# A change of token order inside a batch, so that three rows of q, k and v lie together for a partition

## The chip, the cores and the metric

The kernel runs on one core of one Trainium2 chip, in one launch. The metric is the device time of that core in microseconds (us), a median over runs. A core has five engines with an instruction stream each: TensorE (PE in the profile, with its weight loads as PEld), VectorE (DVE), ScalarE (ACT), GpSimd (POOL) and SyncE (SP). In this kernel SP issues every DMA, one after the other, in the order of its instruction stream; its rows are called SPq.

## The reference

Attention over 4 batches of 12 heads, 448 tokens and 64 dimensions, and then two feed-forward layers on 1792 tokens of 768 features. Cut to what matters:

```python
q_n, k_n = rmsnorm(q, g_q), rmsnorm(k, g_k)          # over the 64 dimensions of a head
scores = q_n @ k_n.transpose(0, 1, 3, 2) / sqrt(64)   # 448 x 448 for each head
attn = softmax(scores)
x = (attn @ v).transpose(0, 2, 1, 3).reshape(1792, 768)
h = x @ w_in                                          # 768 -> 2048
x = (h * sigmoid(1.702 * h)) @ w_out                  # 2048 -> 768
h = x @ w_in2
out = (max(h, 0) + alpha * min(h, 0)) @ w_out2
```

All is in float32. A token's row of the output depends on the tokens of its batch through a sum over keys, so the tokens of a batch may stand in any order as long as q, k and v have the same one and the output rows go back to their places.

## The kernel before

Products are formed from float16 halves: a float32 value becomes a high and a low part, and three matmuls (high by high, high by low, low by high) stand for one. The work goes by pairs of heads, 6 pairs in a batch (NP), 24 in all; P counts them.

For a pair, `load_qk` (L312) brings q and k of both heads into one tile `qk` of 128 partitions by 7 places by 2 heads by 64 numbers. 448 tokens are three and a half blocks of 128, so k takes places 0 to 2 and the lower half of place 3, and q the upper half of place 3 and places 4 to 6. Token 128c + p lies in place c on partition p. A head needs four DMAs (three blocks of k, the rest of k, three blocks of q, the rest of q), a pair eight. In batches 1 to 3 the second head's q begins 64 tokens late and ends with its first 64. `load_v` (L329) brings v in five DMAs: three blocks, the last 64 rows, and the first 64 rows once more. `normalize` (L350) squares on ACT (`sq`, L362), sums and takes the inverse root on DVE, and scales on DVE for the first eight pairs and on POOL for the rest (L379, L380). `prep_pair` (L383) makes the high and the low half (`hl`, L393 on ACT, L394), and one DMA transpose (L399) turns them into `t1`, in which tokens run along the columns. For batches 1 to 3 it also splits v into `vs` and copies two pieces of it to other partitions (L413, L414).

A pair has four units of up to 128 query rows for each head. `scores` (L450, tile `sp`, two buffers in PSUM) is followed by the row maximum on DVE (`nm`, L452) and the exponential on ACT (`pr`, L461). In batch 0 the probabilities are turned by float32 matmuls with a diagonal (`tp`, L494) and copied out by ACT (`ptf`, L497). In batches 1 to 3 they are split into halves (`ph`, L479 on ACT, L502 on DVE) and turned by DMA transposes (L508) into `pt`. The fourth unit of a pair has 64 rows of each head in one tile. `values` (L525, tile `xp`) multiplies by v; in batch 0 the second half of a pair goes in three parts of 192, 128 and 64 columns for each block of keys, in the other batches in two.

The stages follow each other in time. The first stage runs the first two units of all six pairs of batch 0, between the loading and conversion of the first weights (`weights`, L180, loads at L200, conversions at L132, L148, L149, splits at L163, L164). `first_x` and `first_in` (L620) then begin the first layer for batch 0, while the last two units of each pair follow. Then the first layer's second half (`yp`, L690) and the batches 1 to 3 (`hp`, L667) run on PE, with the attention of the next batch woven in by a fixed pace (L1094 to L1105). The second layer (`h`, L775, and `op`, L931) and the stores (L923) end the program. `v_scale` (L279) reads all of v of a batch in eight loads (`vst`) for a common scale; for batch 1 it is called at step 8 (VS_AT) of the second loop over batch 0, L1075.

What sets the order on each engine is a scheduler that simulates the program when it is built: each engine's stream is then fixed. So an edit that shortens one thing moves others too.

## Time and profile before

| | us |
|---|---|
| median of 3 runs | 1238.12 (1235.25 to 1238.38) |
| the profiled execution | 1238.87, span 1237.1 |
| PE busy | 1091.2 (88% of the span) |
| DVE busy | 845.0 (68%) |
| ACT busy | 708.2 (57%) |
| POOL busy | 84.1 (7%) |
| DMA queue that SP issues to | 302480 packets, 159.45 MB, 50.4% of the time of 16 DMA engines |

The span is the time from the first instruction to the last. PE's share is an average over stages with different limits: in the slices of the page it is at nine tenths or more from the middle of the program on, and far below that at the beginning. Busy time doesn't count the issuing of DMAs, so SP has no line in the table; its issues stand in the timeline as SPq rows with a start and a length.

### The profile page before, as it was taken

To read this page: it belongs to the slowest core of one execution; us is meant where nothing else is said; L and a number is where in the kernel's file an instruction comes from. 1 tells how busy PE (TensorE), PEld (TensorE's weight loads), DVE (VectorE), ACT (ScalarE), POOL (GpSimd) and SP (SyncE) were. 2 spreads that over 40 slices of the span, in tenths; PEclk is the share of its full clock that TensorE was granted. 3 is DMA by queue.
4 is the path that set the end of the run, shared out by engine and by line. 5 is a ranking of instruction groups with operands and counts; after the bars stand their busy time and mean duration, and the time that the engine had idled before them with its cause. 6 is when DMAs were issued, how large, how long until landed. Compare 5 with 4: busy or idle time off the path is not lost.

```text
span 1237.1 us, 18887 instructions
## 1 busy us (share of the span) xinstructions
PE 1091.2 (88%) x6877; PEld 615.3 (50%) x6877; DVE 845.0 (68%) x1594; ACT 708.2 (57%) x1447; POOL 84.1 (7%) x54
## 2 busy tenths in 40 slices
PE   0564589976988889899999999799999999999998
PEld 0332357765544444445545555444444458666665
DVE  6988868899666687646764295749997334777441
ACT  2673767787567776656876256236766535565220
POOL 0000000032122123211100000000000000000000
PEclk9886789997999999899999999999999999999999
DMA  6784724466677757675655470346534214352200
GB/s 161 201 217 134 185 78 121 113 115 120 140 153 145 146 116 155 131 124 107 117 99 106 144 263 1 115 176 221 198 134 165 75 73 139 115 165 93 69 33 32
DMA packets 302573, 160.65 MB, mean 130 GB/s; under 512 B 240272, under 2 KB 285840, under 8 KB 302480
## 3 DMA queue, kind: packets, MB, share of 16 engines
q1 hardware_dynamic: 302480, 159.45, 50.4%
q8 instruction: 54, 0.88, 0.3%
q14 instruction: 39, 0.32, 0.1%
HBM read 92.02 MB, written 25.69 MB: 95 GB/s over the span
## 4 chain that ended last, share of the span: by engine, by line
PE 53%; DVE 20%; DMA 11%; ACT 8%; issue 5%; SPq 4%; DVEq 0%; ACTq 0%
PE op L931 15%; PE yp L690 12%; PE h L775 9%; PE hp L667 7%; PE xp L525 4%; PE sp L450 3%; DVE nm L452 2%; ACT pr L461 2%; PE tp L494 2%; PE hp L620 2%; DVE ph L502 2%; DMA t<-hl 2%; DMA g<-in_moe_w_in_dram 1%; DVE g L125 1%; DMA g<-in_moe_w_out_dram 1%
## 5 line engine op out<-in xcount | busy, mean ns | idle before, releaser
L690 PE MATMUL yp<-g,w1o 128*128 128x448 f16 x1152 | 231.1, 359 | 0.5 <-DVE g L125 0.3
L775 PE MATMUL h<-x,w2i 128*128 128x512 f16 (+1 forms) x1152 | 218.9, 352 | 0.9 <-ACT neg L782 0.9
L667 PE MATMUL hp<-x,w1i 128*128 128x448 f16 x864 | 172.6, 358 | 2.5 <-ACT x L124 1.6
L690 PEld LDWEIGHTS <-w1o 128*128 128x128 f16 x1152 | 111.7, 99 | 116.7 <-issue 19.8
L775 PEld LDWEIGHTS <-w2i 128*128 128x128 f16 x1152 | 112.6, 98 | 106.1 <-issue 1.2
L667 PEld LDWEIGHTS <-w1i 128*128 128x128 f16 x864 | 83.2, 99 | 86.8 <-issue 14.0
L461 ACT ACTIVATE pr<-sp,nm,c_s 128x448 f32<-128x448 f32 x168 | 120.3, 719 | 2.0
L502 DVE SCALAR_TENSOR_TENSOR ph<-pr,sm,ph 128x448 f16<-128x448 f32 x126 | 95.2, 782 | 19.7 <-ACT ph L479 19.6
L450 PE MATMUL sp<-t 64*128 64x448 f16 (+1 forms) x480 | 61.3, 364 | 42.5 <-ACT pr L461 21.2
L452 DVE TENSOR_REDUCE nm<-sp 128x2 f32<-128x896 f32 x96 | 92.5, 964 | 7.8 <-PE sp L450 7.4
L931 PEld LDWEIGHTS <-even 128*128 128x128 f16 x672 | 65.7, 98 | 43.1
L479 ACT ACTIVATE ph<-pr,sm 128x448 f16<-128x448 f32 x126 | 77.8, 659 | 14.8 <-DVE sm L470 13.4
L783 DVE SCALAR_TENSOR_TENSOR pos<-neg,nalpha,pos 128x512 f32<-128x512 f32 (+1 forms) x64 | 43.5, 681 | 61.0 <-ACT neg L782 60.8
L781 ACT ACTIVATE pos<-h 128x512 f32<-128x512 f32 (+1 forms) x64 | 34.4, 538 | 70.6 <-PE h L775 66.4
L494 PE MATMUL tp<-dg,pr 128*128 128x128 f32 x336 | 56.6, 328 | 15.1 <-ACT sq L362 7.5
L620 PE MATMUL hp<-x,w1i 128*128 128x256 f16 (+1 forms) x576 | 62.1, 266 | 7.3 <-DVE t L632 4.2
L931 PEld LDWEIGHTS <-odd 128*128 128x128 f16 x504 | 49.3, 98 | 32.6
L125 DVE SCALAR_TENSOR_TENSOR g<-t,ratio_w1o,g 128x448 f16<-128x448 f32 x64 | 51.4, 805 | 20.4 <-ACT g L124 20.0
L931 PE MATMUL op<-w2lo,even 128*128 128x384 f16 x384 | 63.5, 326 | 0.0
L494 PEld LDWEIGHTS tp<-dg,pr 128*128 128x128 f32 x336 | 50.4, 233 | 25.3 <-issue 10.9
L620 PEld LDWEIGHTS <-w1i 128*128 128x128 f16 x576 | 53.3, 101 | 15.4 <-issue 11.6
L362 ACT ACTIVATE sq<-qk 128x448 f32<-128x448 f32 x48 | 27.3, 574 | 57.2 <-DMA qk<-in_k_dram 29.0
(201 smaller groups left out, 1606.1 us busy)
## 6 DMA issues: line engine op xcount, KB each, us to landing
g<-in_moe_w_in_dram SPq DMA_DIRECT2D x24, 512.0 KB, 5.2
g<-in_moe_w_out_dram SPq DMA_DIRECT2D x32, 384.0 KB, 3.8
w2raw<-in_moe_w_in_dram SPq DMA_DIRECT2D x24, 512.0 KB, 5.3
w2raw<-in_moe_w_out_dram SPq DMA_DIRECT2D x16, 768.0 KB, 6.3
g_dram<-pos SPq DMA_DIRECT2D x48, 256.0 KB, 2.0
gp<-g_dram SPq DMA_DIRECT2D x8, 1024.0 KB, 6.7
odd<-g_dram SPq DMA_DIRECT2D x6, 1024.0 KB, 5.5
y_dram<-y SPq DMA_DIRECT2D x24, 224.0 KB, 2.3
```

The source lines that it names most:

```text
L125: nc.vector.scalar_tensor_tensor(out=dst[1], in0=src, scalar=scale, in1=dst[0], op0=ALU.mult, op1=ALU.subtract)
L450: nc.tensor.matmul(out=dst, lhsT=lhsT, rhs=kt[ds, 0:S], start=(i == 0), stop=(i == 2))
L452: nc.vector.tensor_reduce(out=nm[:, 0:n], in_=sp[:, 0:n, 0:S], op=ALU.max, axis=AX, negate=True)
L461: nc.scalar.activation(out=pr[i], in_=sp[:, i, 0:S], func=AF.Exp, bias=nm[:, i:i + 1], scale=c_s, accum_out=sm[:, i:i + 1])
L479: nc.scalar.activation(out=ph[:, i, 0:S], in_=pr[i], func=AF.Copy, scale=sm[:, i:i + 1])
L494: nc.tensor.matmul(out=tp[:, c, i], lhsT=pr[i][:, o:o + 128], rhs=ph[:, i], start=True, stop=True)
L502: nc.vector.scalar_tensor_tensor(out=ph[:, i, S:2 * S], in0=pr[i], scalar=sm[:, i:i + 1], in1=ph[:, i, 0:S], op0=ALU.mult, op1=ALU.subtract)
L620: nc.tensor.matmul(out=ps, lhsT=w1i[:, kk, e, m * 128:(m + 1) * 128], rhs=xs[0, kk][:, f, cols], start=(i == 0), stop=(i == 3 * KD - 1))
L667: nc.tensor.matmul(out=ps, lhsT=w1i[:, kk, e, m * 128:(m + 1) * 128], rhs=x[:, f], start=(n == 0), stop=(n == 3 * KD - 1))
L690: nc.tensor.matmul(out=ps, lhsT=w1o[:, m, e, j * 128:(j + 1) * 128], rhs=g[:, m, f], start=(n == 0), stop=(n == 3 * KF - 1))
L775: nc.tensor.matmul(out=ps, lhsT=w2i[:, kk, e, m * 128:(m + 1) * 128], rhs=x2[kk][:, f], start=(c == 0), stop=(c == 3 * KD - 1))
L931: nc.tensor.matmul(out=ps, lhsT=ops[:, o, m, f], rhs=rhs[:, e], start=(c == 0), stop=(c == 3 * KH - 1))
```

## The change

Three rows of a batch that lie together in memory, 3p, 3p + 1 and 3p + 2, go to places 0, 1 and 2 of partition p; the last 64 rows keep their order in place 3. For this the tiles of q, k and v have the head ahead of the place. One DMA then brings the three blocks of k for both heads, in runs of 192 numbers where there were runs of 64. A pair has four loads for q and k and three for v. The second head's q is no longer shifted. Then the fourth unit of a pair has to go to two places in `pt`, and its transpose becomes two, of 64 rows each. The store puts each row back, with a step of three rows in memory, and a store that spans two places becomes two. In batch 0 the second half of `values` has two parts of 192 columns. The eight loads of `v_scale(1)` may issue only after the transpose of the last pair of batch 0.

```diff
+    def main_rows(src, b, p):
+        return src[b, 2 * p:2 * p + 2, 0:ST].rearrange("h (p c) d -> p h (c d)", c=3)
+    def some_rows(src, b, p, first, step=1):
+        return src[b, 2 * p:2 * p + 2, first:first + 64 * step:step].rearrange("h s d -> s h d")
     def load_qk(P):
-        qk = raw_p.tile([128, NT2, 2, D], F32, tag="qk", name="qk", bufs=QKB)
-        for h in range(2):
-            o = 64 if b and h else 0
-            kh, qh = k[b, 2 * p + h], q[b, 2 * p + h]
-            nc.sync.dma_start(out=qk[:, 0:3, h], in_=kh[0:ST].rearrange("(c p) d -> p c d", p=128))
-            nc.sync.dma_start(out=qk[0:64, 3, h], in_=kh[ST:S])
-            nc.sync.dma_start(out=qk[:, 4:7, h], in_=qh[o:o + ST].rearrange("(c p) d -> p c d", p=128))
-            nc.sync.dma_start(out=qk[64:128, 3, h], in_=qh[0:64] if o else qh[ST:S])
+        qk = raw_p.tile([128, 2, NT2, D], F32, tag="qk", name="qk", bufs=QKB)
+        places = qk.rearrange("p h c d -> p h (c d)")
+        nc.sync.dma_start(out=places[:, :, 0:3 * D], in_=main_rows(k, b, p))
+        nc.sync.dma_start(out=places[:, :, 4 * D:], in_=main_rows(q, b, p))
+        nc.sync.dma_start(out=qk[0:64, :, 3], in_=some_rows(k, b, p, ST))
+        nc.sync.dma_start(out=qk[64:128, :, 3], in_=some_rows(q, b, p, ST))
     def load_v(P):
-        for c in range(3):
-            nc.sync.dma_start(out=vr[:, c], in_=vb[c * 128:(c + 1) * 128])
+        nc.sync.dma_start(out=vr.rearrange("p h c d -> p h (c d)")[:, :, 0:3 * D], in_=main_rows(v, b, p))
         h = 0 if b else 64
-        nc.sync.dma_start(out=vr[h:h + 64, 3], in_=vb[384:448])
-        nc.sync.dma_start(out=vr[64 - h:128 - h, 3], in_=vb[0:64])
+        nc.sync.dma_start(out=vr[h:h + 64, :, 3], in_=some_rows(v, b, p, ST))
+        nc.sync.dma_start(out=vr[64 - h:128 - h, :, 3], in_=some_rows(v, b, p, 0, 3))
...
-            side.tensor_tensor(out=ks, in0=ks, in1=gs.unsqueeze(2).to_broadcast([128, 4, 2, D]), op=ALU.mult)
+            side.tensor_tensor(out=ks, in0=ks, in1=gs.unsqueeze(1).to_broadcast([128, 2, 4, D]), op=ALU.mult)
...
-        hl = att_p.tile([128, 2, n * 128], F16, tag="hl", name="hl", bufs=HLB)
-        nc.scalar.activation(out=hl[:, 0], in_=flat, func=AF.Copy)
+        hl = att_p.tile([128, 2, n, 2, D], F16, tag="hl", name="hl", bufs=HLB)
+        nc.scalar.activation(out=hl[:, 0], in_=qk, func=AF.Copy)
...
-        nc.sync.dma_start(out=vs[0:64, 4:7], in_=vs[64:128, 0:3])
-        nc.sync.dma_start(out=vs[64:128, 4:7], in_=vs[0:64, 1:4])
+        nc.sync.dma_start(out=vs[0:64, :, 4:7], in_=vs[64:128, :, 0:3])
+        nc.sync.dma_start(out=vs[64:128, :, 4:7], in_=vs[0:64, :, 1:4])
...
-    PARTS0 = (((0, 0, 0, 256), (1, 256, 0, 256)), ((0, 0, 256, 192), (1, 256, 256, 128), (1, 192, 384, 64)))
+    PARTS = (((0, 0, 0, 256), (1, 256, 0, 256)), ((0, 0, 256, 192), (1, 192, 256, 192)))
...
-        for i in range(n):
-            nc.sync.dma_start_transpose(out=pts[P, half][:, :, slots[i]], in_=ph[:, i])
+        for i in range(2):
+            nc.sync.dma_start_transpose(
+                out=pts[P, half][:, :, cols[i]:cols[i] + 64 * n], in_=ph[:, i] if n == 2 else ph[64 * i:64 * i + 64, 0]
+            )
...
         def store(i, k):
-            nc.sync.dma_start(out=out[p * 256 + i * 128:p * 256 + (i + 1) * 128, k * H2:(k + 1) * H2], in_=ob[:, i, k])
+            r = 0
+            while r < 128:
+                b, at = divmod(p * 256 + i * 128 + r, S)
+                c, at = divmod(at, 128)
+                n = min(128 - r, 128 - at if c < 3 else 64)
+                o, step = (b * S + 3 * at + c, 3) if c < 3 else (b * S + ST, 1)
+                nc.sync.dma_start(out=out[o:o + (n - 1) * step + 1:step, k * H2:(k + 1) * H2], in_=ob[r:r + n, i, k])
+                r += n
...
             if i == VS_AT:
-                v_scale(1)
+                with tc.issue_after(moved[NP - 1].ins):
+                    v_scale(1)
```

Over the program SP has 647 rows of instructions where it had 757: 144 loads fewer, 18 transposes and 16 stores more. The line numbers of the changed kernel differ; its loads are at L328 to L331 and L343 to L346, its transposes at L402 (`hl`) and L510 (`ph`). The order on SP changes in three places that matter for what follows.

The first is SP's very beginning: the end of the loads of pair 0, the two gains `gq` and `gk`, and the first load of pair 1. Before:

```order
L325 DMA qk<-in_q_dram 128x3x64
L326 DMA qk<-in_q_dram 64x64
L340 DMA w1o<-in_v_dram 128x2x64 x3
L342 DMA w1o<-in_v_dram 64x2x64
L343 DMA w1o<-in_v_dram 64x2x64
L258 DMA gq<-in_g_q_dram 128x64
L259 DMA gk<-in_g_k_dram 128x64
L323 DMA qk<-in_k_dram 128x3x64
```

Now, from the first DMA of the program on:

```order
L328 DMA qk<-in_k_dram 128x2x192
L329 DMA qk<-in_q_dram 128x2x192
L330 DMA qk<-in_k_dram 64x2x64
L331 DMA qk<-in_q_dram 64x2x64
L343 DMA w1o<-in_v_dram 128x2x192
L345 DMA w1o<-in_v_dram 64x2x64
L346 DMA w1o<-in_v_dram 64x2x64
L258 DMA gq<-in_g_q_dram 128x64
L259 DMA gk<-in_g_k_dram 128x64
L328 DMA qk<-in_k_dram 128x2x192
```

The second gain was the program's 15th DMA and is its 9th; the first load of the weights, behind pair 1, was the 29th and is the 17th.

The second place is SP in the first stage, around the transposes of batch 0 (`w1o<-hl`: the first weights' second tile holds `t1` of the first pairs for a while). Before, at the transpose of pair 3:

```order
L200 DMA g_151<-in_moe_w_in_dram 128x1024
L399 DMA_TRANSPOSE w1o<-hl 128x14x128
L200 DMA g_151<-in_moe_w_in_dram 128x1024 x3
L340 DMA v_569<-in_v_dram 128x2x64 x3
L342 DMA v_569<-in_v_dram 64x2x64
L343 DMA v_569<-in_v_dram 64x2x64
```

Now, at the transposes of pairs 2 and 3:

```order
L200 DMA g_139<-in_moe_w_in_dram 128x1024 x9
L200 DMA g_139<-in_moe_w_out_dram 128x4x192
L402 DMA_TRANSPOSE w1o<-hl 128x14x128
L328 DMA qk<-in_k_dram 128x2x192
L329 DMA qk<-in_q_dram 128x2x192
L330 DMA qk<-in_k_dram 64x2x64
L331 DMA qk<-in_q_dram 64x2x64
L200 DMA g_139<-in_moe_w_out_dram 128x4x192
L402 DMA_TRANSPOSE w1o<-hl 128x14x128
```

All 24 loads of the first weights now stand ahead of the transpose of pair 2, and so does the first load of the second weights; the transposes of pairs 4 and 5 stand behind 12 and 14 more of the latter, and the eight `vst` loads, which stood among the weight loads ahead of pair 4, follow right behind pair 5.

The third place is SP in the middle of the program, behind the transpose of one pair in the shadow of the first `yp`. Before:

```order
L399 DMA_TRANSPOSE t1_3875<-hl_3872 128x14x128
L413 DMA vs_3718<-vs_3718 64x384
L414 DMA vs_3718<-vs_3718 64x384
L340 DMA vr_3827<-in_v_dram 128x2x64 x3
L342 DMA vr_3827<-in_v_dram 64x2x64
L343 DMA vr_3827<-in_v_dram 64x2x64
L699 DMA y_dram_72<-y_3845 128x448
L508 DMA_TRANSPOSE pt_3869<-ph_3773 128x7x128 x2
L508 DMA_TRANSPOSE pt_3869<-ph_3849 128x7x128
L508 DMA_TRANSPOSE pt_4005<-ph_3921 128x7x128 x2
L325 DMA qk_4066<-in_q_dram 128x3x64
```

Now:

```order
L402 DMA_TRANSPOSE t1_3762<-hl_3759 128x14x128
L414 DMA vs_3611<-vs_3611 64x2x192
L415 DMA vs_3611<-vs_3611 64x2x192
L343 DMA vr_3716<-in_v_dram 128x2x192
L345 DMA vr_3716<-in_v_dram 64x2x64
L346 DMA vr_3716<-in_v_dram 64x2x64
L703 DMA y_dram_72<-y_3732 128x448
L510 DMA_TRANSPOSE pt_3756<-ph_3666 128x7x128
L328 DMA qk_4229<-in_k_dram 128x2x192
L510 DMA_TRANSPOSE pt_3756<-ph_3666 128x7x128
L510 DMA_TRANSPOSE pt_3756<-ph_3736 128x7x64 x2
L510 DMA_TRANSPOSE pt_3893<-ph_3808 128x7x128 x2
```

The order is the same in kind, with fewer loads between the transposes and one transpose more in each pair (128x7x64 twice for what was one of 128x7x128).

## Rows read from the trace of the kernel before

**Rows 1.** Stretches: length; busy (xcount) PE, PEld, DVE, ACT, POOL; clock; DMA share; GB/s

```profile
0.00:16.00 16.00, 0.00 (x0) 0.00 (x0) 6.48 (x30) 2.90 (x4) 0.70 (x6) 1.00 0.37 83
32.00:175.00 143.00, 82.88 (x405) 52.90 (x406) 122.05 (x273) 88.89 (x188) 0.00 (x0) 0.77 0.64 172
175.00:248.00 73.00, 72.69 (x578) 54.78 (x579) 56.94 (x136) 52.83 (x136) 0.00 (x0) 1.00 0.44 105
248.00:325.00 77.00, 58.52 (x564) 43.76 (x563) 69.67 (x149) 60.27 (x143) 22.48 (x13) 0.89 0.64 121
325.00:500.00 175.00, 149.80 (x1023) 74.62 (x1022) 121.72 (x241) 118.13 (x274) 39.92 (x24) 0.96 0.73 143
500.00:700.00 200.00, 199.70 (x1364) 101.38 (x1364) 107.60 (x197) 123.72 (x287) 21.03 (x12) 0.98 0.56 106
```

**Rows 2.** Waits of PE, 325 to 500: sum in us, times, longest

```profile
PE sp L450 <- ACT pr L461: 18.2, 8, 4.4
```

**Rows 3.** Waits of ACT, 325 to 500

```profile
ACT sq L362 <- DMA qk<-in_k_dram: 14.7, 6, 4.2
ACT sq L362 <- DMA qk<-in_q_dram: 11.7, 6, 3.7
```

**Rows 4.** SP's issues by line, 325 to 500: count, min/median/max length in ns

```profile
L323 SPq DMA_DIRECT2D qk<-in_k_dram x17: 379/584/1744, 329.0 to 496.3; - x17
L324 SPq DMA_DIRECT2D qk<-in_k_dram x17: 487/501/592, 329.6 to 496.9; - x17
L340 SPq DMA_DIRECT2D vr<-in_v_dram x21: 456/467/1697, 349.3 to 486.1; - x21
L342 SPq DMA_DIRECT2D vr<-in_v_dram x7: 673/678/683, 350.9 to 486.6; - x7
L399 SPq DMA_TRANSPOSE t<-hl x7: 1558/1607/1817, 344.4 to 481.4; - x7
L508 SPq DMA_TRANSPOSE pt<-ph x49: 1227/1248/1842, 326.4 to 498.9; - x49
```

**Rows 5.** SP's timeline, 325 to 500: its first row and its last

```profile
324.95 0.58 SPq L325 DMA_DIRECT2D qk<-in_q_dram  x1
...
497.52 2.58 SPq L508 DMA_TRANSPOSE pt<-ph  x2
```

**Rows 6.** SP's timeline at the start: start, length, line, DMA

```profile
9.03 0.43 SPq L259 DMA_DIRECT2D gk<-in_g_k_dram  x1
...
17.02 2.73 SPq L200 DMA_DIRECT2D g<-in_moe_w_in_dram  x5
```

**Rows 7.** DVE's timeline at the start, with idle time before and its releaser

```profile
13.15 0.23 DVE L260 TENSOR_TENSOR gq<-gq,gk 128x64 f32<-128x64 f32 x1 [2.27 <-DMA gk<-in_g_k_dram]
18.03 1.09 DVE L394 TENSOR_TENSOR hl<-qk,hl 128x896 f16<-128x896 f32 x1 [0.49 <-ACT hl L393]
```

**Rows 8.** Timeline: pair 4's transpose on SP, and what it released on PE

```profile
122.62 1.56 SPq L399 DMA_TRANSPOSE t<-hl  x1
...
126.74 2.42 PE L450 MATMUL sp<-t 64*128 64x448 f16 x12 [15.28 <-DMA t<-hl]
```

**Rows 9.** PE's timeline: values of batch 0, first half, 256 columns

```profile
108.23 3.23 PE L525 MATMUL xp<-ptf,w1o 128*64 128x256 f32 x12 [1.20 <-ACT ptf L497]
```

**Rows 10.** Chain of waits, 175 to 248: values of batch 0, second half, three parts

```profile
194.26 3.49 PE xp L525 x24
```

**Rows 11.** DVE by line, 248 to 325: busy, mean ns, idle before and its releaser

```profile
L125 DVE SCALAR_TENSOR_TENSOR g<-t,ratio_w1o,g 128x448 f16<-128x448 f32 x16 | 16.1, 1018 | 6.9 <-ACT g L124 6.8
```

**Rows 12.** DVE by line, 0 to 180: the two multiplies of the preparation

```profile
L380 DVE TENSOR_TENSOR qk<-qk,rs 128x896 f32<-128x896 f32 x8 | 8.4, 1086 | 0.1
L379 DVE TENSOR_TENSOR qk<-qk,gs 128x512 f32<-128x512 f32 x8 | 5.5, 683 | 0.0
```

**Rows 13.** SP's issues of the stores: count, min/median/max in ns

```profile
L923 SPq DMA_DIRECT2D out_dram<-ob x28: 332/332/517, 1050.9 to 1234.2; - x28
```

**Rows 14.** DMAs by line, 325 to 500: count, size, us to landing

```profile
vst<-in_v_dram SPq DMA_DIRECT2D x16, 168.0 KB, 2.8
```

More of the change, by code (lines that the diff above doesn't have):

```diff
@@ L300, in first_tiles @@
                 part[:, 0:a].rearrange("p (c t) -> p c t", t=128),
-                part[:, a:HELD].bitcast(F32).rearrange("p (c h d) -> p c h d", h=2, d=D)
+                part[:, a:HELD].bitcast(F32).rearrange("p (h c d) -> p h c d", h=2, d=D)
             )
-        vr = att_p.tile([128, 11, 2, D], F16, tag="vs", name="v0")
+        vr = att_p.tile([128, 22 * D], F16, tag="vs", name="v0")
         return (
             att_p.tile([128, 2 * NT2, 128], F16, tag="t1", name="t1"),
-            vr[:, 0:2 * NV].rearrange("p c h d -> p (c h d)").bitcast(F32).rearrange("p (c h d) -> p c h d", h=2, d=D)
+            vr[:, 0:4 * NV * D].bitcast(F32).rearrange("p (h c d) -> p h c d", h=2, d=D)
         )
@@ L332, in load_v @@
         b, p = divmod(P, NP)
-        vb = v[b, 2 * p:2 * p + 2].rearrange("h s d -> s h d")
         if b:
-            vr = raw_p.tile([128, NV, 2, D], F32, tag="vr", name="vr")
+            vr = raw_p.tile([128, 2, NV, D], F32, tag="vr", name="vr")
         else:
@@ L398, in prep_pair @@
             t1 = att_p.tile([128, 2 * n, 128], F16, tag="t1", name="t1")
-        moved[P] = nc.sync.dma_start_transpose(out=t1, in_=hl.rearrange("p e n -> p (e n)"))
+        moved[P] = nc.sync.dma_start_transpose(out=t1, in_=hl.rearrange("p e c h d -> p (e c h d)"))
         yield
@@ L407, in prep_pair @@
             return
-        vs = att_p.tile([128, 11, 2, D], F16, tag="vs", name="vs")
-        vflat = vr.rearrange("p c h d -> p (c h d)")
-        hflat = vs[:, 0:4].rearrange("p c h d -> p (c h d)")
-        lflat = vs[:, 7:11].rearrange("p c h d -> p (c h d)")
-        split((hflat, lflat), vflat, av[:, b:b + 1])
-        nc.sync.dma_start(out=vs[0:64, 4:7], in_=vs[64:128, 0:3])
-        nc.sync.dma_start(out=vs[64:128, 4:7], in_=vs[0:64, 1:4])
+        vs = att_p.tile([128, 2, 11, D], F16, tag="vs", name="vs")
+        hi, lo = (vs[:, :, c:c + 4].rearrange("p h c d -> p h (c d)") for c in (0, 7))
+        split((hi, lo), vr.rearrange("p h c d -> p h (c d)"), av[:, b:b + 1])
+        nc.sync.dma_start(out=vs[0:64, :, 4:7], in_=vs[64:128, :, 0:3])
+        nc.sync.dma_start(out=vs[64:128, :, 4:7], in_=vs[0:64, :, 1:4])
         preps[P] = (t1, vs)
@@ L482, in low @@
     def low(u):
-        P, half, slots, _ = unit(u)
+        P, half, cols, place = unit(u)
         pr, sm, ph = probs.pop(u)
@@ L487, in low @@
             if (P, half) not in pts:
-                pts[P, half] = att_p.tile([128, NV, 4, 128], F32, tag="pt", name="ptf")
+                pts[P, half] = att_p.tile([128, NV, 512], F32, tag="pt", name="ptf")
             for h in range(2):
@@ L505, in low @@
         if (P, half) not in pts:
-            pts[P, half] = att_p.tile([128, 7, 4, 128], F16, tag="pt", name="pt")
-        for i in range(n):
-            nc.sync.dma_start_transpose(out=pts[P, half][:, :, slots[i]], in_=ph[:, i])
+            pts[P, half] = att_p.tile([128, 7, 512], F16, tag="pt", name="pt")
+        for i in range(2):
+            nc.sync.dma_start_transpose(
+                out=pts[P, half][:, :, cols[i]:cols[i] + 64 * n], in_=ph[:, i] if n == 2 else ph[64 * i:64 * i + 64, 0]
+            )
     def values(P, half):
@@ L512, in values @@
         vs = preps[P][1]
-        pt = pts.pop((P, half)).rearrange("p c i t -> p c (i t)")
+        pt = pts.pop((P, half))
         if half == 0 or b == 0:
@@ L520, in values @@
             steps = [(c, c, slice(0, 128)) for c in range(7)] + [(c + 7, c, slice(0, 128)) for c in range(4)]
-        parts = (PARTS if b else PARTS0)[half]
+        parts = PARTS[half]
         for group in (parts,) if b else [(part,) for part in parts]:
```

42 lines of the change are left out of this document (21 added, 21 removed).

## The prediction

> **What bounds the kernel now.** I read the stretches first. PE is the engine that ends the program, so what can be won is PE's idle time, and the stretches say where it is [rows 1]. Up to 175 us PE does little: from 32 to 175 it is busy for 82.9 of 143 us, while DVE is busy for 122.1. That stage is DVE's, with 21 us of holes. From 175 to 248 PE is full. From 248 to 325 PE is idle for 18.5 us and DVE busy for 69.7 of 77: DVE again. From 325 to 500 PE is idle for 175 - 149.8 = 25.2 us, and here no computing engine is near its limit (DVE 0.70, ACT 0.68). From 500 to 700 PE is full.
>
> So 325 to 500 needs a second look. PE waits there chiefly for a buffer of scores that ACT's exponential has to free, 18.2 of the 25.2 us [rows 2]. ACT in turn waits 14.7 + 11.7 = 26.4 us, before the squares, for loads of q and k [rows 3]. The loads are late because of the queue that issues them: with the median lengths, k's and q's four lines take 17 x 2 x (0.584 + 0.501) = 36.9 us (q priced like k), v's 21 x 0.467 + 14 x 0.678 = 19.3, the transposes 49 x 1.248 + 7 x 1.607 = 72.4, together 129 of 175 us in these lines alone [rows 4]. Summed over SP's timeline, from its first row to its last, 195 DMAs hold SP for 160 of 175 us [rows 5]. SP has no busy column, but it is the fullest engine of this stretch.
>
> **The change part by part.** I price against the profiled execution, 1238.87 us, which is 0.75 above the median.
>
> *Start, 0 to 32.* The gain gk was SP's 15th DMA, issued at 9.03 [rows 6], and its arrival released DVE at 13.15 [rows 7]. It is now the 9th. Six issues fewer at 0.58 are 3.5 us. The first weight load was the 29th, at 17.02 [rows 6], and is the 17th: 12 x 0.58 = 7 us earlier. DVE was idle for 9.5 of the first 16 us [rows 1]. Pair 0's subtraction at 18.03 [rows 7] need not come earlier itself, since DVE now takes pair 1's sums and the first conversions ahead of it; but that work is then done. I take -3.5, between 0 (pair 0's own loads are first in either order) and -7 (the weights' lead).
>
> *32 to 175.* The work is the same and only its order moves. Ahead of the transposes of pairs 2 to 5 there are now weight loads that wait for DVE, and the vst loads are behind pair 5. Pair 4's transpose took 4.1 us from issue to PE [rows 8], time in which DVE must have other work; the conversions are such work, and cover it. If they don't, each of three bunches (pair 2, 4, 5) costs about 5.5 us with the scores behind it. In the other direction the holes are 21 us, part of them late loads. I take 0, from -8 to +12.
>
> *175 to 248.* PE is full, so each matmul saved counts. Twelve of 256 columns take 3.23 us [rows 9], 0.27 each, so 192 columns should take 0.20. Two pairs' second half in three parts took 3.49 for 24 [rows 10]; in two parts it is 16 x 0.20 = 3.2. That saves 0.27 for two pairs, 0.8 for six. Bounds 0 and 3.5 (24 matmuls fewer at 3.49 / 24 each).
>
> *248 to 325.* DVE is idle for 7.3 us, 6.8 of them before the split of g, behind ACT [rows 1, 11]. Earlier loads may unblock ACT a little: -1.5, from -5 to 0.
>
> *325 to 500.* The main term. A pair's q and k were eight issues, 2 x 2 x (0.584 + 0.501) = 4.34 us, and are four: two large ones at 0.584, and two that carry both heads like v's rest at 0.678, 2.52 us. That is 1.82 less, for 8.5 pairs (17 heads) 15.5 us. v's three blocks at 0.467 become one at 0.584: 0.82 x 7 = 5.7. Against that a fourth unit's transpose becomes two of half the rows. The trace has none of 64 rows. A transpose of twice the blocks takes 1.607 for 1.248, so by that line half takes 1.07, and at worst the full 1.248 [rows 4]: per pair 0.89 to 1.25 more, for seven pairs 6.2 to 8.8. I take the line, the nearest pair of rows. SP is then relieved by 15.5 + 5.7 - 6.2 = 15.0 us of 160. Of PE's idle time 18.2 of 25.2, or 0.72, hangs behind ACT [rows 2], so I take 0.72 x 15.0 = 10.8, rounded to -11. Bounds: -20 (little idle left) and +2 (the extra transposes on the way of the values, and nothing from the loads).
>
> The Trainium skill (DMA: Bandwidth & Descriptors, Anatomy of one DMA) describes a fixed cost of some 2 us for each DMA on the GpSimd path, nearly all of it the wait for the last write's receipt, with only about 50 ns of the sequencer. By that, the 48 issues fewer of this stretch would spare SP next to nothing, and the time would be that of the first rival below. The rows here hold SP for 0.47 to 0.68 us for each load, so I go by them.
>
> *Nothing.* The copies of vs have twice the runs. Reading the tile by heads gives ACT, DVE and POOL runs of 64 numbers; the multiply by rs already has an operand spread over runs of 64, and costs 1.21 ns per column against 1.33 for the one by gs [rows 12]. So strides of this kind cost nothing visible: 0, or at most a tenth of such an operation (0.07 of 0.683 us), which a DVE that is busy for 0.70 after 325 has room for [rows 1]. The stores are 44 for 28, at 0.332 each [rows 13], beside full matmuls, except the last: one issue more at the end, +0.4 (0.3 to 0.9 if it lands later).
>
> Sum: -3.5 + 0 - 0.8 - 1.5 - 11 + 0.4 = -16.4. That gives 1222.5 in the profiled execution, and 0.75 less as a median: 1222 us.
>
> **The rivals.**
>
> *The queue was not it.* SP's release passes to the chain sp, nm, pr, ph, pt, with DMA engines at a share of 0.73 [rows 1], and the loads' waits are filled by others. For it: the transposes are the larger part of SP's time and grow. Against: 26.4 us of ACT's waits name the loads. Then the terms of 248 to 500 vanish and -3.9 is left: 1234.
>
> *The holes close.* The start gives 7, 32 to 175 gives 6 (weight loads no longer queue behind 13 loads a pair), 248 to 325 gives 4, 325 to 500 gives 20: with 0.8 and 0.4 that is -37.4, or 1201 for all together; three quarters of it, 1210, is the likelier form. The Trainium skill (same page, Why small descriptors are slow) says that runs of 256 bytes lose about a quarter on a fixed overhead for each packet, so runs of 768 would relieve the DMA engines too. The share of 0.73 leaves that open; no row prices it.
>
> *The first stage gets longer.* Pairs 2 and 3 stand behind all the first weights, pairs 4 and 5 behind 14 loads of the second, and the eight vst loads, 2.8 us each to land [rows 14] and two at a time, come right before the first layer. If DVE runs out of conversions there, the three bunches cost 16.5 us and the four rounds of vst about 3.4 each less cover, some 7: with -3.5 at the start, +20 at the end of the stage. With the -13 of the later terms that is +7.5: 1246. For it: DVE's order is fixed, so one late transpose stops all behind it. Against: there are weights to convert throughout. It decides if PE's first layer begins over 16 us later than at 175.
>
> *The change doesn't do what it says.* The loads are fewer by the order itself; it could only be that an issue with 256 runs holds SP for longer than one with 384, which is not to be expected from 0.584 (384 runs) against 0.501 (64).
>
> **How the numbers follow.** Forecast 0.52, in its own range 1213 to 1231; queue was not it 0.18; holes close 0.16; first stage longer 0.14. 0.3% of 1238 is 3.7 us, about what a measurement can tell from no change: the bounds are 1234.4 and 1241.8. The first rival lies at the upper of these two ends of faster, so half of it is faster, half the same; the forecast and the closing holes are faster, the long stage slower except for a small part. Faster 0.77, same 0.11, slower 0.12. The range leaves out about a tenth on each side: 1206 to 1241.
>
> **What would show it.** SP's issues in the stretch of the first yp fall from 160 to about 145 us of 175, ACT's waits for q and k from 26 to under 10, and PE's idle time there from 25 to about 14. A transpose of 64 rows takes 1.0 to 1.25 us to issue. DVE's product of the gains starts near 9.7. PE's first hp comes 0 to 8 us before 175. Wrong would be: the waits for q and k gone and PE as idle as before (the first rival), or PE's first hp later than 175 (the third).

## The result, and the profile after

| | us |
|---|---|
| before, median of 4 runs beside it | 1238.25 (1235.25 to 1241.39) |
| after, median of 4 runs | 1227.62 (1225.87 to 1228.48) |
| ratio | 0.9912 (95% interval 0.9885 to 0.9939) |
| the profiled execution of after | 1228.48, span 1226.7 |

The change makes the kernel faster by 10.6 us as a median, and by 10.4 from profiled execution to profiled execution; the forecast was 16.4. The stretches of after, with the columns of [rows 1]:

```profile
0.00:16.00 16.00, 0.00 (x0) 0.00 (x0) 7.20 (x33) 3.96 (x6) 0.70 (x6) 1.00 0.54 163
32.00:175.00 143.00, 86.23 (x468) 54.44 (x468) 123.86 (x280) 90.83 (x196) 0.00 (x0) 0.80 0.58 160
175.00:248.00 73.00, 73.00 (x570) 52.55 (x570) 61.39 (x144) 57.63 (x144) 2.54 (x2) 1.00 0.54 125
248.00:325.00 77.00, 59.54 (x514) 41.91 (x512) 67.75 (x153) 58.26 (x135) 25.94 (x16) 0.89 0.71 137
325.00:500.00 175.00, 156.35 (x1067) 77.56 (x1066) 123.98 (x243) 119.08 (x278) 37.26 (x23) 0.95 0.70 137
500.00:700.00 200.00, 200.00 (x1360) 102.32 (x1359) 107.36 (x184) 122.98 (x280) 13.80 (x8) 1.00 0.55 123
```

From 325 to 500 PE is idle for 18.7 us where it was idle for 25.2. But fixed stretches hide where a gain arose, since in after everything lies earlier. It is better to cut each program at its own stages: PE's first `hp`, its first `yp`, its first `h`, its last `op`. Same columns; before:

```profile
172.70:313.80 141.10, 121.36 (x1094) 93.92 (x1092) 122.23 (x273) 107.12 (x263) 19.62 (x12) 0.94 0.51 109
313.80:823.00 509.20, 476.12 (x3048) 240.83 (x3047) 320.58 (x576) 304.60 (x656) 63.80 (x37) 0.97 0.58 128
823.00:1233.10 410.10, 409.17 (x2333) 227.90 (x2332) 260.23 (x417) 200.67 (x337) 0.00 (x0) 1.00 0.36 122
```

After:

```profile
165.30:306.00 140.70, 123.24 (x1053) 91.54 (x1052) 122.67 (x277) 110.79 (x273) 21.87 (x13) 0.94 0.57 120
306.00:809.20 503.20, 474.90 (x3039) 240.43 (x3039) 318.04 (x569) 299.41 (x643) 57.67 (x35) 0.98 0.56 126
809.20:1222.00 412.80, 409.77 (x2334) 227.98 (x2332) 260.52 (x417) 200.84 (x337) 0.00 (x0) 1.00 0.36 122
```

Read the lengths: the first layer begins 172.7 - 165.3 = 7.4 us earlier, its first half is 0.4 shorter, the middle (first layer's second half, with the attention of batches 1 to 3 beside it) 6.0 shorter, and the second layer 2.7 longer. From the last `op` to the end it is 4.7 us for 4.0. That is -7.4 - 0.4 - 6.0 + 2.7 + 0.7 = -10.4.

Of the middle's length two parts are lost: PE's idle time, and time at the lower clock. A stretch at half clock counts as busy but does half the work (in after, `yp`'s matmuls of 448 columns start 0.373 us apart at the lower clock and 0.189 at the upper), so its loss is length x (1 - granted clock), added up in pieces of some 10 us; an idle moment at the lower clock counts in both parts. Before lost 33.1 + 13.6 us, after 28.3 + 12.0. What is left, the middle's work at full clock, is 462.5 and 462.9, and between 460 and 468 in every kernel below. So the two together account for the middle, and idle time alone doesn't. How they share it is less certain: the run with 28 stores below executes the same instructions up to the end of the middle, and lost 31.6 + 8.5, in sum the same 40.

SP's issues, 325 to 500, to be held against [rows 4]:

```profile
L328 SPq DMA_DIRECT2D qk<-in_k_dram x7: 378/529/537, 326.5 to 477.5; - x7
L329 SPq DMA_DIRECT2D qk<-in_q_dram x7: 426/481/573, 327.5 to 478.0; - x7
L330 SPq DMA_DIRECT2D qk<-in_k_dram x7: 617/627/644, 327.9 to 478.6; - x7
L331 SPq DMA_DIRECT2D qk<-in_q_dram x7: 605/605/1459, 328.6 to 479.2; - x7
L343 SPq DMA_DIRECT2D vr<-in_v_dram x8: 408/546/620, 335.0 to 497.9; - x8
L510 SPq DMA_TRANSPOSE pt<-ph x57: 1188/1248/2536, 329.9 to 493.7; - x57
```

The issue of three blocks is not longer for carrying both heads: 0.529 us for k, where one head took 0.584. That of the rest is: 0.627, where one head took 0.501. And a transpose is not shorter for having half the rows: about a quarter of the 57 have 64 rows, and the shortest of all took 1.188. By medians a pair's q and k fell from 4.34 to 2.24 us of SP, v from 2.72 to 1.80 (the second of v's rests took 0.645 before, and not the 0.678 that the forecast gave both), and the transposes rose by 1.25: 1.78 us less a pair, against 1.82 + 0.82 - 0.89 = 1.75 in the forecast. With the length of every DMA row of SP in the stretch added up one by one, SP is held for 137.8 of 175 us where it was held for 156.2. Part of these 18 us is the cut of the stretch: it holds q and k of 7 pairs now and of 8.5 before, and 10 `vst` loads for 16. (The forecast's 160, from [rows 5], took grouped rows, which hold the gaps between issues too.)

The waits that [rows 2, 3] showed, in after (sum in us, times, longest):

```profile
ACT sq L365 <- DMA qk<-in_q_dram: 19.4, 7, 6.5
PE sp L446 <- ACT pr L460: 11.5, 9, 2.7
```

PE's wait fell by 6.7 us, from 18.2 to 11.5, and ACT's waits for loads by 7.0, from 26.4 to 19.4. SP's timeline (start, length, DMA) shows why there are still late loads:

```profile
378.36 0.53 SPq L328 DMA_DIRECT2D qk<-in_k_dram  x1
378.98 6.81 SPq L510 DMA_TRANSPOSE pt<-ph  x5
385.85 0.57 SPq L329 DMA_DIRECT2D qk<-in_q_dram  x1
386.47 0.63 SPq L330 DMA_DIRECT2D qk<-in_k_dram  x1
387.14 0.60 SPq L331 DMA_DIRECT2D qk<-in_q_dram  x1
387.85 2.72 SPq L510 DMA_TRANSPOSE pt<-ph  x2
390.66 2.51 SPq L402 DMA_TRANSPOSE t<-hl  x1
```

The first load of a pair goes out at 378.4, and the other three only 7 us later, behind five transposes. The square needs all four now.

### The profile page after: what moved, and what is told of

It is laid out like the page before. It is cut to its first block, busy times and chain, and to the rows that moved or that the text cites. A ratio compares the mean times of both kernels' runs of the same rounds, so it can differ in the third digit from the quotient of the medians.

```text
span 1226.7 us, 18612 instructions
## 1 busy us (share of the span) xinstructions
PE 1087.1 (89%) x6829; PEld 608.2 (50%) x6829; DVE 842.5 (69%) x1594; ACT 707.7 (58%) x1447; POOL 80.2 (7%) x54
## 4 chain that ended last, share of the span: by engine, by line
PE 56%; DVE 20%; DMA 11%; ACT 6%; issue 5%; SPq 2%; ACTq 0%; DVEq 0%
PE op L942 16%; PE yp L694 13%; PE hp L671 8%; PE h L779 6%; PE xp L529 5%; PE sp L446 3%; PE hp L624 3%; PE tp L493 2%; DMA yr<-y_dram 2%; DVE nm L451 2%; DVE ph L504 2%; DMA w2raw<-in_moe_w_in_dram 2%; ACT pr L460 1%; DMA vst<-in_v_dram 1%; DVE g L125 1%
## 5 line engine op out<-in xcount | busy, mean ns | idle before, releaser
L671 PEld LDWEIGHTS <-w1i 128*128 128x128 f16 x864 | 82.7, 98 | 86.4 <-issue 12.8
L504 DVE SCALAR_TENSOR_TENSOR ph<-pr,sm,ph 128x448 f16<-128x448 f32 x126 | 101.7, 831 | 25.0 <-ACT ph L478 24.9
L785 ACT ACTIVATE pos<-h 128x512 f32<-128x512 f32 (+1 forms) x64 | 34.5, 539 | 69.9 <-PE h L779 58.5
L446 PE MATMUL sp<-w1o 64*128 64x448 f16 (+1 forms) x96 | 16.2, 462 | 62.0 <-DMA w1o<-hl 55.7
L452 ACT ACTIVATE nm<-nm,c_s 128x2 f32<-128x2 f32 x96 | 28.0, 292 | 63.7 <-DVE nm L451 63.2
L125 DVE SCALAR_TENSOR_TENSOR g<-t,ratio_w1o,g 128x448 f16<-128x448 f32 x64 | 47.2, 741 | 16.0 <-ACT g L124 15.8
L493 PE MATMUL tp<-dg,pr 128*128 128x128 f32 x336 | 51.4, 308 | 5.1 <-DVE dg L473 3.8
```

The costliest lines, as they stand in the source:

```text
L446: nc.tensor.matmul(out=sp[:, j, 0:S] if n == 2 else sp[ds, 0, 0:S], lhsT=qt[ds] if n == 2 else qt[ds, 64:128], rhs=kt[ds, 0:S], start=(i = ...
L493: nc.tensor.matmul(out=tp[:, c, i], lhsT=pr[i][:, o:o + 128], rhs=ph[:, i], start=True, stop=True)
L504: nc.vector.scalar_tensor_tensor(out=ph[:, i, S:2 * S], in0=pr[i], scalar=sm[:, i:i + 1], in1=ph[:, i, 0:S], op0=ALU.mult, op1=ALU.subtract)
L671: nc.tensor.matmul(out=ps, lhsT=w1i[:, kk, e, m * 128:(m + 1) * 128], rhs=x[:, f], start=(n == 0), stop=(n == 3 * KD - 1))
```

## The experiments

The theory is the forecast's: SP's issue time sets the pace of the attention of batches 1 to 3. The rivals are that something else in the change did it (the order of batch 0, the rule for `v_scale(1)`, the larger runs in memory), or that the loads' place in the queue matters and not its fullness. Ratios are to the kernel before, run beside each series, with medians of 1236.8 to 1237.9. Differences between two changed kernels are of their medians; where they come from different series, the difference by the ratios stands beside it, since the kernel before itself moves by 1 to 2 us. Both differences have an uncertainty of several us, as the intervals of the ratios show.

**Loads of batches 1 to 3 cut in two by heads**, 13 a pair again, with runs in memory as long as in after:

```diff
+        hs = [slice(0, 1), slice(1, 2)] if b > 0 else [slice(0, 2)]
+        for hh in hs:
+            nc.sync.dma_start(out=places[:, hh, 0:3 * D], in_=main_rows(k, b, p)[:, hh])
...
```

> The changed kernel with the loads of batches 1 to 3 cut into 13 again, by heads, in the same runs of 768 bytes. If fewer issues on SP made the middle of the program faster, the first layer begins at 165 as in the changed kernel, the first hp of batch 1 comes some 5 us later than its 388, and the time is 1231 to 1234. If the longer runs were the cause (DMA engines), or the middle gained nothing from the loads: 1226 to 1229.

Measured 1237.33, ratio 1.0002 (0.9986 to 1.0018): the whole gain is gone, 9.7 us for 108 loads (11 by the ratios), more than was expected. The middle:

```profile
297.50:819.70 522.20, 480.32 (x3048) 242.88 (x3047) 316.03 (x574) 302.51 (x652) 63.53 (x37) 0.96 0.57 125
```

The first `yp` came 16 us earlier than in the kernel before, and all of it was lost in a middle of 522 us: 41.9 idle, 20.3 to the lower clock. SP was held for 158.6 of 175 us (row by row, as above). What waited for it, 325 to 500:

```profile
ACT sq L370 <- DMA qk<-in_q_dram: 22.1, 10, 6.4
PE sp L451 <- ACT pr L465: 13.4, 7, 5.8
PE xp L534 <- DMA pt<-ph: 6.1, 5, 3.5
ACT ph L483 <- DMA pt<-ph: 5.8, 3, 3.2
```

ACT's wait for loads is hardly longer than in after. New are the last two rows: the transposes are late (PE waits 6.1 us for them, in after 1.1). PE is idle there for 28.6 us, 10 more than in after, and this row is half of it. So a load costs also by what stands behind it in the queue. The length of the middle overstates the price: it began 8.5 us earlier than in after and ended 10.5 later.

It also answers the Trainium skill (DMA: Bandwidth & Descriptors, Why small descriptors are slow), by which runs of 256 bytes lose about a quarter. Here the runs of 768 bytes stayed and the gain went. The cleaner pair is the last run below, with as many loads and transposes in batches 1 to 3 as the kernel before and longer runs: its middle is 508.4 us for 509.2. So longer runs by themselves show no gain in time there.

**Loads of batch 0 cut in two by heads** (the same edit with `b == 0`):

> The changed kernel with the loads of batch 0 alone cut into 13 again. If the start of the program is where the loads paid, the first layer begins at 172 to 176 instead of 165 and the time is 1233 to 1237. If the middle made the gain: 1227 to 1230.

Measured 1229.61, ratio 0.994 (0.9922 to 0.9957). The first layer begins at 169.6, 4.3 us later than in after, but the end is only 2.0 later (3.5 by the ratios).

**One transpose for the fourth unit:**

```diff
-        for i in range(2):
+        if half == 1:
+            cols = (0, 128) if n == 2 else (256,)
+        for i in range(n):
             nc.sync.dma_start_transpose(
-                out=pts[P, half][:, :, cols[i]:cols[i] + 64 * n], in_=ph[:, i] if n == 2 else ph[64 * i:64 * i + 64, 0]
+                out=pts[P, half][:, :, cols[i]:cols[i] + 128], in_=ph[:, i]
```

> The changed kernel with one transpose of 128 rows for the fourth unit, as before (it leaves the probabilities of that unit in the wrong columns). If SP's issue time is what the middle waits for, seven issues of some 1.1 us less give 3 to 5 us: 1223 to 1225. If the queue's order and not its fullness makes q and k late: 1226 to 1229.

Measured 1219.72, ratio 0.986 (0.984 to 0.988): 7.9 us (6.4 by the ratios), more than the 3 to 5 expected, for 18 issues, which hold SP for 18 x 1.25 = 22.5 us. This kernel leaves the fourth unit's probabilities in the wrong columns. The middle is 497.8 us, 5.4 less than in after. It lost 29.2 to idle time and 5.1 to the clock, in sum 34.3 where after lost 40.3 (28.3 + 12.0). That would make it all the clock's, but against the second execution of after's order (31.6 + 8.5) both fall; which of the two it is can't be told from single profiles. How they hang together is seen from 430 to 440 (columns as above), first in the run with 13 loads, then in this one; the two stretches hold different work:

```profile
430.00:440.00 10.00, 5.26 (x32) 2.60 (x31) 8.68 (x15) 8.24 (x19) 6.31 (x3) 0.62 0.92 139
```

```profile
430.00:440.00 10.00, 8.69 (x61) 4.45 (x56) 8.14 (x21) 7.50 (x17) 3.33 (x2) 1.00 0.55 110
```

In the first PE was idle for 4.7 of 10 us, and the granted clock, which is either 2.4 or 1.2 GHz, averages 0.62; in the second it was idle for 1.3, and the clock stayed at 1.00.

**`v_scale(1)` without its rule:**

```diff
-                with tc.issue_after(moved[NP - 1].ins):
-                    v_scale(1)
+                v_scale(1)
```

> The changed kernel without the rule that holds the eight loads for the scale of batch 1 back. If the loads alone make the first stage shorter: 1226 to 1230. If putting the scale's eight loads and reductions off is what brings the first layer forward: it begins 3 to 5 us later and the time is 1230 to 1233.

Measured 1228.39, ratio 0.9925 (0.9907 to 0.9944): within 1 us of after (1.6 by the ratios). The rule does nothing that shows.

**Loads of batches 1 to 3 issued by ScalarE:**

```diff
-        nc.sync.dma_start(out=places[:, :, 0:3 * D], in_=main_rows(k, b, p))
+        eng = nc.scalar if b > 0 else nc.sync
+        eng.dma_start(out=places[:, :, 0:3 * D], in_=main_rows(k, b, p))
...
```

> The changed kernel with the loads of q, k and v of batches 1 to 3 issued by ScalarE (ACT) and not by SP; nothing else is edited. Theory: SP's issue time bounds the attention of batches 1 to 3; 18 pairs x (4 x 0.53 + 3 x 0.6) = some 70 us leave SP, which then has under 90 of 175 us; the waits of the squares for q (24.6 us from 317 to 490) go. But ACT, busy for 0.68 of that stretch, now pays for issues itself, in order with its exponentials: 1212 to 1225. Rival A, lateness is the order of one queue and not its fullness: the same, since the loads then stand behind ACT's own waits: 1224 to 1232. Rival B, ACT becomes the bound: 1235 and more, with the waits of PE's scores for the exponential over 20 us in that stretch.

Measured 1224.03, ratio 0.989 (0.9859 to 0.9921): 3.6 us below after (2.7 by the ratios). ACT's waits for q and k from 325 to 500 fall to 4.3 us, SP is held for 117.1 us, 20.7 less than in after, and the middle is 501.6, only 1.6 less. The time is at the upper end of what the theory gave and the lower end of rival A's. Either little hung on SP's fullness any more, or the issues took back from ACT what they gave; this run can't tell which.

**The same loads issued by GpSimd** (`nc.gpsimd` for `nc.scalar`):

> The changed kernel with the loads of q, k and v of batches 1 to 3 issued by GpSimd (POOL). POOL is busy for 0.23 of the stretch from 325 to 500 with the scaling of q and k and for less elsewhere. Theory (SP's issue time bounds that stretch): as with ScalarE but without its price, 1208 to 1220, squares' waits for q from 24.6 to under 8 us. Rival A (chain of scores, exponential, transposes bounds it): 1224 to 1230. Rival B (a load issued by POOL lands so late or holds POOL so long that the scaling gets late): 1232 and more.

Measured 1228.60, ratio 0.993 (0.991 to 0.9951). The theory missed: it gave 1208 to 1220, and the time is that of rival A. ACT's waits for q fall to 6.2 us and SP is held for only 113.6 us, with no gain; the middle is 513.8, 10.6 longer than in after:

```profile
301.60:815.40 513.80, 480.15 (x3105) 243.36 (x3105) 338.27 (x591) 316.19 (x686) 120.34 (x122) 0.98 0.59 129
```

(The profiled execution, 1233.47, is one of the longest of ten, 1226.83 to 1234.08.) From 325 to 500 POOL is busy for 71.5 us (37.3 in after), and transposes land 3.7 us after their issue (3.0 in after). What the loads cost may have moved there; no run separates it.

**Loads given as more urgent to the scheduler:**

```diff
-                    load_qk(P + 1 + QKB)
-                    load_v(P + 3)
+                    with tc.high_priority(400):
+                        load_qk(P + 1 + QKB)
+                        load_v(P + 3)
```

> The changed kernel with the loads of q, k and v of batches 1 to 3 given to the scheduler as more urgent, so that they stand earlier on SP, ahead of transposes which wait for their probabilities. As many DMAs as before the edit. If the loads are late because of their place in the queue and not because the queue is full: 1217 to 1224, with the squares' waits for q under 15 us from 317 to 490. If it is SP's fullness alone: 1225 to 1230, since what the loads gain the transposes lose.

Measured 1229.04 (1222.24 to 1231.29), ratio 0.992 (0.9888 to 0.9953). The profiled execution is the shortest of the six. From 325 to 500:

```profile
ACT sq L365 <- DMA qk<-in_q_dram: 8.3, 5, 2.6
PE sp L446 <- ACT pr L460: 7.5, 6, 3.2
PE xp L529 <- DMA pt<-ph: 5.3, 4, 2.7
```

The wait for loads falls by 11 us and PE's wait for ACT by 4.0, PE's wait for the transposes rises by 4.2, and the middle stays at 502.9 us. The queue's order only changes who waits.

**28 stores:**

```diff
-            r = 0
-            while r < 128:
...
+            nc.sync.dma_start(out=out[p * 256 + i * 128:p * 256 + (i + 1) * 128, k * H2:(k + 1) * H2], in_=ob[:, i, k])
```

> The changed kernel with 28 stores of 128 rows as before the change, in place of 44; the rows then go to wrong places of the output. If the stores' extra 16 issues and their strided rows cost something at the end: 0.4 to 3 us less, 1224 to 1227, with the time from the last matmul to the end shorter by that. If they are hidden: 1227 to 1229, no difference.

Measured 1224.96 (1222.53 to 1231.89), ratio 0.9904 (0.987 to 0.9938): its runs enclose those of after, so this is inconclusive. From the last `op` to the end it takes 3.9 us for 4.7, the 0.8 that the stores cost. In its profile the second layer already begins at 805.1 (809.2 in after), ahead of any store, with the same instructions in the same order on every engine up to there. So this is a second execution of after's order. The first layer begins at 162.2 in it (165.3), the first `yp` at 302.0 (306.0), and the middle and PE's wait of 325 to 500 are:

```profile
302.00:805.10 503.10, 471.52 (x3040) 239.24 (x3040) 318.27 (x569) 299.35 (x644) 58.11 (x35) 0.98 0.55 126
```

```profile
PE sp L446 <- ACT pr L460: 15.7, 9, 3.1
```

The middle is as long as in after. The wait that fell from 18.2 to 11.5 is 15.7 here, and PE's idle time from 325 to 500 is 21.4 us for 18.7. About 4 us is what two executions of the same work can differ by, and single profiles are to be read with that in mind.

**A ring order of the columns.** The fourth unit lies in one piece when place 3 stands between places 0 and 1 for both heads. A quarter of the values then goes to two strips of 128 columns, and the stores follow the new order:

```diff
-    UNITS = ((0, (0, 256), 4), (0, (128, 384), 5), (1, (0, 192), 6), (1, (128, 320), 3))
-    PARTS = (((0, 0, 0, 256), (1, 256, 0, 256)), ((0, 0, 256, 192), (1, 192, 256, 192)))
+    UNITS = ((0, (0, 256), (5, 4)), (0, (128, 384), (6, 6)), (1, (0, 256), (4, 5)), (1, (128,), (3,)))
+    PARTS = (((0, 0, 192, 256), (1, 256, None, 256)), ((0, 0, 0, 192), (1, 192, 128, 192)))
...
+    def far(x):
+        return bass.AP(x.tensor, x.offset, [list(x.ap[0]), [320, 2], [1, 128]])
...
-        for i in range(2):
+        for i in range(n):
+            nc.sync.dma_start_transpose(out=pts[P, half][:, :, cols[i]:cols[i] + 128], in_=ph[:, i])
```

> The changed kernel with the tokens of batches 1 to 3 in a ring order of columns: place 0, place 3, place 1, place 2. The fourth unit of a pair then lies in one piece again, so that one DMA transpose of 128 rows does it (126 transposes of probabilities, not 144), and the output rows still go to their places. As many matmuls; a quarter of the values goes to two strips of 128 columns. Theory: the 18 more transposes, at 1.25 us of SP each, are the cost that the change brought, and this gives back what the run with one transpose showed: 1218 to 1222, PE's idle time and its stretches at the lower clock between 320 and 520 us below those of the changed kernel. Rival (the gain of that run came from elsewhere, or two strips cost PE time): 1225 to 1230.

Measured 1214.86 (1213.51 to 1218.93), ratio 0.9828 (0.9786 to 0.987): 12.8 us below after (10.4 by the ratios), and the fastest version here. By the profiles, 15.0 us apart, the middle is 7.6 us shorter and the first layer's first half 2.8; the other 4.6 lie outside the transposes of the probabilities: 1.8 before the first layer, 1.8 in the second layer, 1.0 at the end, where there are 40 stores for 44. The middle:

```profile
301.40:797.00 495.60, 469.01 (x3045) 238.95 (x3045) 312.54 (x571) 301.85 (x651) 59.53 (x36) 0.99 0.57 129
```

SP is held for 135.0 of 175 us, PE's waits for ACT's exponential from 325 to 500 are 8.0 us, and the lower clock costs 6.8. Two strips cost nothing: 22 matmuls of values over 256 columns, half of them into two strips here, take 1.39 us in both.

**The ring order, and the loads by ScalarE:**

> The ring order, and the loads of q, k and v of batches 1 to 3 issued by ScalarE. If both ease the same queue, little is left for the second: 1216 to 1222, and not the sum of the two gains (8 + 3.6, 1216) but within 3 us of the ring order alone. If SP is still what PE waits for: 1210 to 1216. If ScalarE's issues cost: above the ring order alone.

Measured 1223.56, ratio 0.9885 (0.9852 to 0.9918): 8.7 above the ring order. The first layer's first half, then the middle:

```profile
166.60:313.10 146.50, 119.99 (x1032) 90.39 (x1030) 122.95 (x274) 106.02 (x257) 20.13 (x12) 0.93 0.53 111
313.10:806.70 493.60, 471.71 (x3063) 239.72 (x3062) 313.13 (x572) 302.47 (x657) 60.51 (x36) 0.99 0.61 130
```

SP is held for 105.7 us, 29 less than in the ring order, and the middle is 2.0 us shorter, but the first half is 8.6 longer (26.5 us idle for 16.2). The relief of SP won little in the middle, and in a stage that waits for ACT and DVE its issues do harm; that it is ACT's own time is inferred, since the rows name DVE and the sequencer as PE's releasers there.

**The gains ahead of pair 0's loads, in the kernel before:**

```diff
+        gains()
         load_qk(0)
```

> The kernel before, with the loads of the two gains ahead of pair 0's loads; nothing else. The forecast's term for the start, -3.5 us, rested on the gain gk landing some six issues earlier. If that is what starts DVE earlier and the rest of the first stage follows: 1234 to 1236, with PE's first layer beginning 2 to 4 us earlier than at 172.7. If the first layer's earlier start in the changed kernel (165.3) comes from the fewer loads of batch 0 and the earlier weights, or if what is won there is lost by the middle: 1237 to 1239 at the end.

Measured 1233.33, ratio 0.9967 (0.9949 to 0.9985). The first layer begins at 170.0, 2.7 us earlier, the first `yp` 10.9 earlier at 302.9, and the end 3.4 (median) to 6.8 (profile) earlier. The middle, with SP as full as before (154.8 us), is 4.0 us longer: part of a gain ahead of the middle is lost in it.

**The ring order with 13 loads a pair** in batches 1 to 3 (the first edit on the ring order):

> The ring order, with the loads of q, k and v of batches 1 to 3 cut into 13 a pair again: against the ring order it differs by 6 loads a pair, 108 in all, and has no more transposes than the kernel before. It prices the fewer loads by themselves. Theory, by the forecast's terms (15.5 + 5.7 us of SP in the stretch from 325 to 500, times 0.72 of PE's idle time): 15 us above the ring order, 1230. If loads and transposes fill one queue and each microsecond of it costs the same, as the changed kernel with 13 loads showed (9.7 us for 108 loads): 1224 to 1226. If the loads cost only on top of the 18 extra transposes, because only then SP is full: under 1220.

Measured 1224.64 (1221.63 to 1225.87), ratio 0.9886 (0.9864 to 0.9907): 9.8 us above the ring order (7.2 by the ratios). The middle is 508.4 us, SP held for 151.8. Against the kernel before, with as many loads and transposes in these batches, it is 12.8 us faster: all of that arose before the middle, which begins 14.0 us earlier (299.8) and is 0.8 shorter.

Side by side, sorted by how long SP is held from 325 to 500 (us; all but the median from the profiles):

| kernel | SP held | middle | idle | lower clock | median |
|---|---|---|---|---|---|
| after, loads cut | 158.6 | 522.2 | 41.9 | 20.3 | 1237.3 |
| before | 156.2 | 509.2 | 33.1 | 13.6 | 1236.8 to 1238.3 |
| before, gains first | 154.8 | 513.2 | 34.5 | 11.9 | 1233.3 |
| ring, loads cut | 151.8 | 508.4 | 34.1 | 13.6 | 1224.6 |
| after, urgent loads | 143.7 | 502.9 | 30.5 | 8.5 | 1229.0 |
| after | 137.8 | 503.2 | 28.3 | 12.0 | 1227.6 |
| after, 28 stores | 137.6 | 503.1 | 31.6 | 8.5 | 1225.0 |
| after, batch 0's loads cut | 136.6 | 505.8 | 32.3 | 10.2 | 1229.6 |
| ring | 135.0 | 495.6 | 26.6 | 6.8 | 1214.9 |
| after, one transpose | 133.1 | 497.8 | 29.2 | 5.1 | 1219.7 |
| after, without the rule | 128.8 | 499.0 | 30.7 | 6.8 | 1228.4 |
| after, loads by ScalarE | 117.1 | 501.6 | 25.2 | 10.1 | 1224.0 |
| after, loads by GpSimd | 113.6 | 513.8 | 33.6 | 11.9 | 1228.6 |
| ring, loads by ScalarE | 105.7 | 493.6 | 21.9 | 6.9 | 1223.6 |

The middle is long, 508 to 522 us, where SP is held for over 150 of 175 us. Below 144 us its length no longer follows SP: it runs from 493.6 to 505.8, and with the loads on GpSimd it is 513.8.

## Why the prediction was right, and where it was off

*What bounds the kernel.* Right for the loads: SP's issues cost time. Cutting the same 108 loads costs 9.7 us in one order and 9.8 in the other (11 and 7.2 by the ratios), and neither the rule for `v_scale(1)` nor the longer runs account for it. Nor did the transfers get slower: transposes land 3.1 us after their issue in before, 3.0 in after, 3.2 with the loads cut. A pair gives SP back 1.78 us, where 1.75 were forecast. The Trainium skill's 50 ns of sequencer for a DMA (DMA: Bandwidth & Descriptors, Anatomy of one DMA; told there of the GpSimd path) would have left these loads without a price; SP's rows of 0.48 to 0.63 us a load hold. "The queue was not it", 1234, is thereby out. That SP's fullness still bounds the middle after the change is not shown: with the loads on ScalarE and GpSimd it is held for 20.7 and 24.2 us less, and the time fell by 3.6 us and not at all.

*The link from the queue to PE.* Right in kind, and incomplete. The forecast said that late loads hold up ACT, and ACT holds up PE. ACT's waits for loads fell by 7.0 us and PE's wait for ACT by 6.7 (2.5 by the second execution of the same order), while PE's own wait for the transposes was 1.6 and is 1.1. But ACT's waits were expected under 10 us and were 19.4; and where they did fall to 8.3, with urgent loads, PE's wait for ACT fell by 4.0 and its wait for the transposes, now behind the loads on the same queue, rose by 4.2. So a load's wait reaches PE in part, and what a load makes late behind it is a second path, which the forecast had in no term.

*325 to 500, -11.* Too large: the middle gave 6.0 (4.8 idle, 1.6 clock; the two can change places from one execution to the next). The step that failed is the one factor of 0.72 for every microsecond of SP; two sizes were wrong by it. The loads, 21.2 x 0.72 = 15.3, are worth 9.7 or 9.8 by the cut ones. The extra transposes, 6.2 x 0.72 = 4.5, cost 7.9 by the run with one transpose (6.4 by the ratios), and some 10 by the ring order, counting only the middle and the half ahead of it. So the price of a microsecond depends on what is issued: over the program, 18 pairs x 2.91 us = 52 us of load issues (medians of the two ring orders) are worth 0.19 us each, 22.5 us of transpose issues 0.35 (0.14 and 0.28 by the ratios). A transpose stands in the chain from `ph` to `xp`, and a load can go out ahead of its need; that this is the reason is argued, not shown. Whether it depends on fullness too stays open: the loads on other engines gained little, but those engines had to issue them. The price of a 64-row transpose, 1.07, was too low, at the worst end that was given, 1.25.

*Start, -3.5, and 32 to 175, 0.* Too small: the first layer begins 7.4 us earlier in after, and what arises before the middle is worth 12.8 us at the end in the ring order with cut loads. The mechanism came in part: gk is issued at 5.78, 3.25 us earlier, but the product that waits for it comes at 11.30, 1.85 earlier (13.15 in [rows 7], 9.7 forecast), and pair 0's subtraction at 18.62 (18.03). The first weight load is issued at 11.29, 5.7 us earlier, where 7 were forecast.

```profile
11.30 0.23 DVE L260 TENSOR_TENSOR gq<-gq,gk 128x64 f32<-128x64 f32 x1 [2.65 <-DMA gk<-in_g_k_dram]
```

The gains alone, in the kernel before, bring the product to 5.25 and the first layer 2.7 us forward; cutting batch 0's loads takes 4.3 back. At the end these two are worth 3.4 and 2.0 us (3.5 by the ratios). Where the rest of the 12.8 comes from (the longer runs of batch 0, the new order on each engine) no run separates. Pair 4's transpose still releases PE late, but after a shorter idle time (15.28 in [rows 8]):

```profile
129.93 2.42 PE L446 MATMUL sp<-t 64*128 64x448 f16 x12 [8.13 <-DMA t<-hl]
```

So "the first stage gets longer" did not come: PE's first `hp` was at 165.3, just outside the 0 to 8 us before 175 that the forecast gave, on the good side.

*175 to 248, -0.8.* Right in its price, forecast 3.2 us for 16 matmuls:

```profile
184.83 3.24 PE L529 MATMUL xp<-ptf,w1o 128*64 128x192 f32 x16
```

*248 to 325, -1.5.* The wait that it rested on went as hoped, 6.8 us in [rows 11] to 0.2, but PE was idle for 17.5 us after 18.5; the first layer's first half as a whole gave 0.4 where this term and the last had 2.3. A wait gone on DVE was not one that PE ended on.

```profile
L125 DVE SCALAR_TENSOR_TENSOR g<-t,ratio_w1o,g 128x448 f16<-128x448 f32 x16 | 13.2, 841 | 0.2 <-ACT g L124 0.2
```

*Nothing, and the stores.* The strides cost nothing (L382 takes 685 ns for the 683 of [rows 12]), and the tail 0.7 for 0.4. The second layer's +2.7 was in no term. 2.0 of it is PE's wait for ACT there, 2.9 us for 0.9 in before:

```profile
PE h L779 <- ACT neg L786: 2.9, 3, 1.7
```

The other changed kernels took 411.0 to 413.4 us for their second layer, before 410.1. So it isn't this one execution alone; why that wait grew stays open.

Over the sum by profiles, the start was 3.9 us better than forecast, 175 to the middle's end 1.9 + 5.0 worse, the second layer and the tail 3.0 worse. The medians tell it in three steps: 12.8 gained before the middle, 9.8 by fewer loads (ring orders), 12.8 given back from the ring order to after, chiefly by 18 more transposes. They are steps from one kernel to the next, so their sum, 9.8, is the difference of the ends and no test of the parts. The forecast had 5.8, 15.3 and 4.5 for these, so its errors partly cancel, and that the time lies well inside the range is in part luck. "The holes close", 1201 to 1210, is out by the time.
